# Later value loads, output ids behind the branch, a hint on the branch, and expert weights one load earlier

## The chip, the core and the metric

The kernel runs on one core of a Trainium2 chip. TensorE (PE), VectorE (DVE), ScalarE (ACT), GpSimd (POOL) and SyncE (SP) are its engines; each has its own instruction stream, and they wait for each other by semaphores. SP issues the loads of q, k and v, POOL issues the loads of expert weights and the gathers and scatters of token rows. The metric is the device time of one execution in microseconds, the median of the runs; lower is better.

## The reference

Two stages follow each other. The first is causal attention over 4 batches, 8 heads, 768 positions and 64 dimensions, in which a query sees the 96 latest positions and 8 global ones, with a linear bias in the distance. The second is a balanced mixture of 8 experts over the 3072 rows of 512 values that attention gives:

```python
logits = x @ w_gate
order = np.argsort(-logits.flatten())        # all (token, expert) pairs, best first
for idx in order:                            # greedy
    tok, e = int(idx) // E, int(idx) % E
    if assigned[tok] >= 0 or counts[e] >= cap:
        continue                             # cap = 3072 / 8 = 384
    assigned[tok] = e
    counts[e] += 1
for e in range(E):
    mask = assigned == e
    out[mask] = np.maximum(x[mask] @ w1[e], 0.0) @ w2[e]     # 512 -> 1024 -> 512
```

Each token goes to exactly one expert, and each expert has exactly 384 tokens.

## The kernel before

**Attention, 0 to about 125 us.** The work is cut into eight units (a batch and four heads) and sixteen half-units n (a pair of heads). The order of all its instructions is written out by hand in two lists, `PROLOGUE` and `ORDER` (L540 to L560), of steps such as `S1` (scores), `BI`, `EX` (bias, exponential), `AV0` and `AV1` (the two parts of P times V, L405) or `KT`, `QT` (transposes of raw k and q). Raw q and k of a unit land in one of five slots (`load`, L264); v of a half-unit, in one of four (`load_v`, L272: five DMAs, 420 KB). All go through SP's queue in the order in which the lists reach them. A v slot is free again when `AV1` of its half-unit is done, and the load of half-unit n + 4 is written right behind it (L619).

**Routing, about 125 to 159 us.** Four rounds assign most pairs; `dispatch` then turns each token's expert and rank into lists of ids by matmuls with one-hot matrices: `idi` (L916, L930), by which rows are gathered from the token rows in DRAM, and `ido` (L925, L933, L934), by which results are scattered. `fill` puts matmuls of no use between them. A flag `fm` (L937) says whether the rounds left something over, so that the general path is needed; it isn't for these inputs. All engines read it and branch over the general path (L1194, L1195). The gathers of expert 0 are issued ahead of the branch, those of expert 1 behind it.

**Experts, from about 159 us.** Per expert e there are three slabs of 128 tokens. A slab is gathered (`gather`, L1086, nine slots `xe`), transposed by PE (`pxe`, L1107) and copied to SBUF by DVE (`xT`, L1112). The hidden layer is 32 matmuls (`ph`, L1136; expert 0 by slabs, L1126), ACT's relu writes `hT` (L1139), the output layer is 8 matmuls for each slab (`po`, L1169), DVE copies it to one of four `ot` (L1173), and POOL scatters it to `out_dram` (L1174). Behind expert 0's and e's hidden layer the slabs of the next expert are transposed between the slabs of the output layer. The weights of experts 0 to 2 are loaded earlier; `late_weights` (L707) issues w1 and w2 of experts 3 to 7, 1 MB each, one at each expert, two at expert 0 (L1144, L1146), behind the gathers of expert e + 2. A scheduler sets the order between engines' independent instructions here, while `keep_in_program_order` pins what the code marks. In the tables below, s0, s1, ... are the scatters in order, three for an expert.

Of the kernel before, what the change touches and what calls it, by code (L numbers as in the profile page):

```python
# [9 lines left out]
FP32 = mybir.dt.float32  # L10
# [10 lines left out]
DM = H_ * D_  # L21
# [18 lines left out]
TOP = 64  # L40


@with_exitstack
def kernel(
# [173 lines left out]
    with ExitStack() as actx:  # L218
# [342 lines left out]
        VLOAD = {"S0:0": 1, "S1:0": 2, "S2:0": 3}  # L561
        pss = {}
# [14 lines left out]
        def step(op, u):  # L577
# [36 lines left out]
            elif k == "AV":  # L614
                if op[2] == "0":
                    attend(n, (0, 1, 2, 3), 0)
                else:
                    attend(n, (2, 3, 4, 5, 6), 1)
                    if n + NB < 2 * NU:  # L619
                        load_v(n + NB)  # L620
# [39 lines left out]
        with tc.manual_schedule():  # L660
# [4 lines left out]
            nc.sync.dma_start(wg_sb, moe_w_gate.rearrange("(kc p) e -> p kc e", p=128))  # L665
# [5 lines left out]
            load("q", 1)  # L671
            load_v(0)
# [44 lines left out]

    idi = consts.tile([128, NCHUNK], I32)
    ido = consts.tile([128, NCHUNK], I32)
    fm = consts.tile([1, 1], FP32)  # L720

    def routing(general):
      with ExitStack() as dctx:
        dap = dctx.enter_context(tc.tile_pool(name="dap", bufs=1))
        ohp = dctx.enter_context(tc.tile_pool(name="ohp", bufs=1))
# [142 lines left out]
        def dispatch(d0=()):  # L868
# [29 lines left out]
            OH = ditp.tile([128, NCHUNK, NCHUNK], FP16, tag="OH", name="OH")  # L898

# [7 lines left out]
            ohl_of = []  # L907
            for q_, m in enumerate((6, 6, 6, 4, 2)):
                ohl = ohp.tile([128, 128, m], FP16, tag=f"ohl{q_}", name=f"ohl{q_}")
                c0 = len(ohl_of)  # L910
                nc.vector.tensor_tensor(out=ohl, in0=iota_m[:, :, 0:m], in1=bc_m(lo[:, c0 : c0 + m], 128), op=ALU.is_equal)
                ohl_of += [ohl[:, :, i] for i in range(m)]
                if c0:
                    fill(1)
                for c in range(c0, c0 + m):
                    nc.tensor.matmul(pI, lhsT=ohl_of[c], rhs=OHr[:, :, c], start=(c == 0), stop=(c == NCHUNK - 1))  # L916
            assert not toks0 and (general or not toksA and not toksD), (toksA, toksD)
            if general:
                take(OH, ohl_of)
# [8 lines left out]
            for dst, src in ((idi, pI), (ido, pO)):  # L928
                if dst is idi:
                    nc.vector.tensor_scalar(out=idi, in0=src, scalar1=float(N_TOK // 2), scalar2=0.0, op0=ALU.add, op1=ALU.max)  # L930
                else:
# [302 lines left out]
```

## Time and profile before

| | |
|---|---|
| median of 3 runs | 265.55 us (265.2, 265.55, 265.85) |
| profiled execution | 265.26 us |
| its span, first to last instruction | 263.3 us |
| PE, DVE, ACT, POOL busy | 90%, 56%, 58%, 58% |
| mean granted clock of PE | 0.969 of full speed |
| POOL's DMA queue (software_dynamic) | 26.22 MB, 49.5% of 16 engines' span |
| SP's DMA queue (hardware_dynamic) | 22.50 MB, 31.6% |
| instruction DMAs (q8 and q14) | 39 packets, 0.50 MB |

The time is that of the whole execution; the profile's times count from its first instruction. Busy shares are means over three stages with different limits. A chain of waits goes back from the last instruction to what released each step; "issue" in it is time in which an engine waited for nothing that the profile shows. The granted clock is given as a share of 2.4 GHz, so 0.50 is 1.2 GHz. The kernel's inputs are the same in every run, so the branch goes the same way each time.

### The profile page before, as it was taken

What the parts mean: (1) busy time and instruction counts of PE and PEld (TensorE: products, weight loads), DVE (VectorE), ACT (ScalarE), POOL (GpSimd) and SP (SyncE); (2) the same over time, 40 slices, a digit from 0 to 9 for tenths busy, and PEclk for the clock granted to TensorE, in tenths of its full rate; (3) what the DMA queues carried; (4) which work ended last, traced back from release to release, by engine and by line L of the source; (5) the groups of instructions that cost most, each with busy time, mean ns of one, the idle gap of its engine ahead of it and who ended that gap; (6) DMA issues with size and microseconds to landing.
All of it is one profiled execution on the core that took longest, in us unless ns stands there. A gap on an engine that the chain in (4) does not pass through costs nothing. (4 is left out here: it accounts for less than half of the span.)

```text
span 263.3 us, 6939 instructions
## 1 busy us (share of the span) xinstructions
PE 236.5 (90%) x2746; PEld 166.5 (63%) x2757; DVE 147.7 (56%) x330; ACT 153.4 (58%) x301; POOL 153.6 (58%) x285
## 2 busy tenths in 40 slices
PE   8599899799998999999788895999999499999991
PEld 3477778587786888877677664755655245555550
DVE  3999989488898966564878851232121323141320
ACT  1858899399889898464889811532505023505230
POOL 6546948849939989978210027881677572222412
PEclk9889999799999999999999999999999689999998
DMA  6999999764573499999997524599999999417803
GB/s 244 332 415 262 217 250 303 180 175 89 176 128 82 76 179 202 205 181 190 210 213 191 184 77 112 106 200 227 259 234 181 266 257 177 174 40 150 191 21 119
DMA packets 49895, 49.22 MB, mean 187 GB/s; under 512 B 29377, under 2 KB 41409, under 8 KB 49857
## 3 DMA queue, kind: packets, MB, share of 16 engines
q0 software_dynamic: 15712, 26.22, 49.5%
q1 hardware_dynamic: 34144, 22.50, 31.6%
q8 instruction: 23, 0.38, 0.6%
q14 instruction: 16, 0.12, 0.1%
HBM read 56.05 MB, written 9.44 MB: 249 GB/s over the span
## 5 line engine op out<-in xcount | busy, mean ns | idle before, releaser
L1139 ACT ACTIVATE hT<-ph 128x384 bf16<-128x384 f32 x56 | 27.5, 491 | 56.7 <-PE ph L1136 56.2
L365 DVE SCALAR_TENSOR_TENSOR P<-Dm,ps 128x432 f32<-128x432 f32 x92 | 49.2, 598 | 10.1 <-PE ps L347 10.1
L372 ACT ACTIVATE P<-P 128x864 f32<-128x864 f32 x48 | 42.7, 923 | 8.2 <-DVE P L365 7.5
L1173 DVE COPY ot<-po 128x512 f32<-128x512 f32 (+1 forms) x24 | 16.1, 675 | 51.8 <-PE po L1169 27.5
L1086 POOL DMA_INDIRECT xe<-x_tok,idi x24 | 24.3, 1014 | 33.9 <-DVE fc L937 20.0
L1174 POOL DMA_INDIRECT out_dram<-ot,ido x24 | 23.8, 990 | 34.7 <-DVE ot L1173 28.8
L384 POOL TENSOR_TENSOR S<-P 128x576 f32<-128x576 f32 (+1 forms) x32 | 38.9, 1215 | 8.3 <-ACT P L372 7.1
L405 PE MATMUL po<-P,v 128*64 128x216 f32 (+6 forms) x576 | 43.3, 300 | 0.1
L405 PEld LDWEIGHTS po<-P,v 128*64 128x64 f32 x576 | 35.9, 141 | 9.9 <-issue 2.6
L287 DVE STREAM_TRANSPOSE arena<-w_early 128x768 f32<-128x768 f32 x32 | 30.0, 958 | 5.1 <-DMA w_early<-in_k_dram 3.5
L1169 PEld LDWEIGHTS <-hT 128*128 128x128 bf16 x200 | 19.4, 101 | 20.7 <-issue 3.3
L295 ACT COPY kA<-arena 128x720 f32<-128x720 f32 (+2 forms) x18 | 23.6, 1340 | 6.0 <-DVE arena L287 6.0
L347 PE MATMUL ps<-qT,kA 32*128 32x216 f32 (+2 forms) x448 | 23.7, 335 | 3.4 <-DVE P L365 1.9
L519 ACT ACTIVATE x<-pw,ri 128x64 bf16<-128x64 f32 x112 | 24.5, 341 | 3.5 <-PE pw L504 3.5
L347 PE MATMUL ps<-arena,kA 32*128 32x216 f32 (+2 forms) x416 | 21.5, 342 | 4.6 <-ACT arena L315 2.7
L347 PEld LDWEIGHTS ps<-qT,kA 32*128 32x128 f32 x448 | 19.7, 185 | 6.0 <-issue 4.8
L347 PEld LDWEIGHTS ps<-arena,kA 32*128 32x128 f32 x416 | 18.3, 190 | 6.9 <-issue 3.7
L1112 DVE COPY xT<-pxe 128x512 bf16<-128x512 bf16 x24 | 9.5, 418 | 23.3 <-PE pxe L1107 18.3
L412 ACT COPY oT<-po 128x384 f32<-128x384 f32 x32 | 14.7, 475 | 13.4 <-PE po L405 13.4
L1169 PE MATMUL po<-w_late,hT 128*128 128x512 bf16 x69 | 18.4, 423 | 0.2
L1136 PE MATMUL ph<-xT,w_late 128*128 128x384 bf16 x96 | 16.1, 326 | 0.0
L422 PE MATMUL t<-S,onesx 128*32 128x192 f32 x256 | 13.7, 332 | 0.0
(186 smaller groups left out, 353.0 us busy)
## 6 DMA issues: line engine op xcount, KB each, us to landing
w_early<-in_k_dram SPq DMA_DIRECT2D x8, 768.0 KB
w_early<-in_q_dram SPq DMA_DIRECT2D x8, 768.0 KB
w_late<-in_moe_w_dram POOLq DMA_DIRECT2D x6, 1024.0 KB, 11.6
v<-in_v_dram SPq DMA_DIRECT2D x32, 180.0 KB
w_early<-in_moe_w_dram POOLq DMA_DIRECT2D x8, 512.0 KB, 8.9
w_last<-in_moe_w_dram POOLq DMA_DIRECT2D x4, 1024.0 KB, 11.0
arena<-in_moe_w_dram POOLq DMA_DIRECT2D x2, 1024.0 KB, 8.7
x_tok<-x SPq DMA_DIRECT2D x2, 768.0 KB
```

The costliest lines, as they stand in the source:

```text
L287: nc.vector.transpose(out=t, in_=raws[kind, u][:, :, 32 * g : 32 * g + 32])
L295: nc.scalar.copy(out=kAs[u % 2][:, g, i0:i1, 8:128].rearrange("p i (c j) -> p i c j", j=NJ), in_=t[:, i0 * NC5 : i1 * NC5, :].rearrange("p ...
L347: nc.tensor.matmul(at(a)[:, o : o + w], lhsT=kA[r, gd, i, :], rhs=qTt[r, gd, KT * i : KT * i + w], start=(gd == 0), stop=(gd == 1), skip_g ...
L365: nc.vector.scalar_tensor_tensor(out=Ps[n][:, 2 * g : 2 * g + 2, t, :], in0=W, scalar=-8.0 * slopes[2 * (n % NPAIR) + t], in1=st[:, 0 : 2 ...
L372: nc.scalar.activation(P, P, AF.Exp, scale=0.125)
L384: nc.gpsimd.tensor_tensor(out=to[:, :, :, 0:OV], in0=P[:, i0 : i0 + m, :, 0:OV], in1=P[:, i0 - 1 : i0 + m - 1, :, KT:QW], op=ALU.add)
L405: nc.tensor.matmul(po[n, bank][64 * t : 64 * t + 64, a - QB * bank : z - QB * bank], lhsT=v7[:, t, i, :], rhs=Ps[n][:, min(i, 5), t, a - q ...
L519: nc.scalar.activation(x[:, 2 * hf + i, 128 * jj + 64 * t : 128 * jj + 64 * t + 64], ps[:, i, 64 * t : 64 * t + 64], AF.Identity, scale=ri ...
L1086: tc.keep_in_program_order(nc.gpsimd.indirect_dma_start(out=xes[s], out_offset=None, in_=x_tok[:, :], in_offset=bass.IndirectOffsetOnAxis( ...
L1139: nc.scalar.activation(hT[:, fc, :], ph, AF.Relu)
L1169: pin(e, nc.tensor.matmul(po[:, lo:hi], lhsT=hT[:, t, fc, :] if e == 0 else hT[:, fc, 128 * t : 128 * t + 128], rhs=w2_of(e)[:, fc, lo:hi] ...
L1174: s = nc.gpsimd.indirect_dma_start(out=out[:, :], out_offset=bass.IndirectOffsetOnAxis(ap=ido[:, TSLAB * e + t : TSLAB * e + t + 1], axis= ...
```

## The change

There are five parts.

1. Loads of v. A table `VNEXT` says behind which `AV1` a v load stands. v4 now follows `AV1` of half-unit 2, not 0; v5 that of 3, v6 that of 4, v7 and v8 that of 5, and so on, up to v15 behind 11, where it was. The load of the gate weights `wg_sb` moves behind q1.
2. Output ids. The 24 matmuls for `ido` and DVE's two instructions on them leave `dispatch` and stand behind the branch: 14 matmuls ahead of the first slab's transposes, 10 behind them. The fillers there and those between the matmuls are dropped.
3. The branch. The general path is the block that is preferred as fallthrough, and a hint for its branch, "LikelyTaken", is marked for PE, DVE, ACT and POOL in `dispatch`. In the built program the hint is the first instruction of these four engines' programs, more than 300 ahead of the branch, and the few instructions of the other side stand behind the general path instead of ahead of it.
4. The first slab's copy to `xT` is ACT's.
5. The first half of w1 of expert 4 is loaded ahead of expert 1's gathers, the second half and w2 of expert 4 behind them; the second `late_weights` at expert 0 goes. Each later load so stands one step earlier.

```diff
+        VNEXT = {2: (4,), 3: (5,), 4: (6,), 5: (7, 8), 6: (9,), 7: (10,), 8: (11,), 9: (12, 13), 10: (14,), 11: (15,)}
...
                     attend(n, (2, 3, 4, 5, 6), 1)
-                    if n + NB < 2 * NU:
-                        load_v(n + NB)
+                    for m in VNEXT.get(n, ()):
+                        load_v(m)
...
-            nc.sync.dma_start(wg_sb, moe_w_gate.rearrange("(kc p) e -> p kc e", p=128))
             load("k", 1)
...
             load("q", 1)
+            nc.sync.dma_start(wg_sb, moe_w_gate.rearrange("(kc p) e -> p kc e", p=128))
             load_v(0)
...
+    def late_half(hf):
+        m, e = lates[0]
+        assert m == 0
+        tc.keep_in_program_order(nc.gpsimd.dma_start(
+            w1_of(e)[:, 2 * hf : 2 * hf + 2, :],
+            moe_w1[e].rearrange("(kc p) f -> p kc f", p=128)[:, 2 * hf : 2 * hf + 2, :]))
+        if hf:
+            lates.pop(0)
...
+            if not general:
+                tc.mark_branch_hint_location("general", "LikelyTaken", engines=HINT)
...
-            pO = ps_d.tile([128, NCHUNK], FP32, tag="pr", name="pO")
-            for c in range(NCHUNK):
-                if c % 6 == 0:
-                    fill(2)
-                nc.tensor.matmul(pO, lhsT=ohl_of[c], rhs=OH[:, :, c],
-                                 start=(c == 0), stop=(c == NCHUNK - 1))
...
                     if e == 0 and t == 0:
-                        pw = ps_o.tile([128, DM], FP32, tag="po", name="pw")
-                        for i in range(2):
-                            pin(0, nc.tensor.matmul(pw, lhsT=ident_bf, rhs=w1_of(0)[:, 0, 0:DM], start=(i == 0), stop=(i == 1)))
-                    nc.vector.tensor_copy(out=xT_of[e][:, :, t, :], in_=pxe)
+                        out_ids(14, NCHUNK)
+                        pin(0, nc.scalar.copy(out=xT_of[e][:, :, t, :], in_=pxe))
+                    else:
+                        nc.vector.tensor_copy(out=xT_of[e][:, :, t, :], in_=pxe)
...
+            def out_ids(c0, c1):
+                for c in range(c0, c1):
+                    pin(0, nc.tensor.matmul(pO, lhsT=ohl_of[c], rhs=OH[:, :, c], start=(c == 0), stop=(c == NCHUNK - 1)))
+
+            def ido_out():
+                idf = fp.tile([128, NCHUNK], FP32, tag="idf", bufs=1, name="idf")
+                pin(0, nc.vector.tensor_scalar(out=idf, in0=pO, scalar1=float(N_TOK // 2), scalar2=0.0, op0=ALU.add, op1=ALU.max))
+                pin(0, nc.vector.tensor_scalar(out=ido, in0=idf, scalar1=float(N_TOK - 1), scalar2=None, op0=ALU.min))
...
                 late_weights()
-                if e == 0:
-                    late_weights()
-                if e == 0:
-                    pw = ps_h.tile([128, 512], FP32, tag="ph", name="pw")
-                    for i in range(3):
-                        pin(0, nc.tensor.matmul(pw, lhsT=ident_bf, rhs=w1_early[:, 0, 0, 0:512], start=(i == 0), stop=(i == 2)))
...
                 if e == 0:
+                    out_ids(0, 14)
                     load_x(0, (0,))
+                    ido_out()
...
-    with tc.If(flag > 0, preferred_fallthrough_block=False):
+    with tc.If(flag > 0, preferred_fallthrough_block=True, label="general"):
         routing(True)
+    late_half(0)
     gather(1)
+    late_half(1)
+    late_weights()
     experts()
```

POOL's program from the branch on, before: six gathers (three for expert 1, three for expert 2) stand ahead of the first two weight loads, which are w1 and w2 of expert 4.

```order
249 L1195 UNCONDITIONAL_BRANCH
250 L1086 DMA xe_3209<-x_tok,idi 128x512
251 L1086 DMA xe_3213<-x_tok,idi 128x512
252 L1086 DMA xe_3217<-x_tok,idi 128x512
253 L1086 DMA xe_3230<-x_tok,idi 128x512
254 L1086 DMA xe_3234<-x_tok,idi 128x512
255 L1086 DMA xe_3238<-x_tok,idi 128x512
256 L714 DMA w_late_1930<-in_moe_w_dram 128x4x1024
257 L714 DMA w_late_1931<-in_moe_w_dram 128x8x512
258 L1086 DMA xe_3446<-x_tok,idi 128x512
```

And after it; `128x2x1024` is half of w1 of expert 4.

```order
249 L1205 UNCONDITIONAL_BRANCH x2
250 L725 DMA w_late_1930<-in_moe_w_dram 128x2x1024
251 L1089 DMA xe_3123<-x_tok,idi 128x512
252 L1089 DMA xe_3127<-x_tok,idi 128x512
253 L1089 DMA xe_3131<-x_tok,idi 128x512
254 L725 DMA w_late_1930<-in_moe_w_dram 128x2x1024
255 L718 DMA w_late_1931<-in_moe_w_dram 128x8x512
256 L1089 DMA xe_3147<-x_tok,idi 128x512
257 L1089 DMA xe_3151<-x_tok,idi 128x512
258 L1089 DMA xe_3155<-x_tok,idi 128x512
259 L718 DMA w_late_1932<-in_moe_w_dram 128x4x1024
260 L1184 DMA out_dram<-ot,ido 3072x512
```

The first half has moved ahead of expert 1's gathers, the rest of expert 4's weights ahead of expert 2's, and w1 of expert 5 ahead of expert 3's gathers and of the first scatter.

SP's loads at the start of the second slots' use, before (`v7_0` and `v7_1` are the slots that take v4 and v5 here; the q and k are of later units).

```order
31 L268 DMA w_early_99<-in_q_dram 128x1536
32 L277 DMA v7_0_137<-in_v_dram 120x6x64
33 L279 DMA v7_0_137<-in_v_dram 8x7x64
34 L277 DMA v7_0_137<-in_v_dram 120x6x64
35 L279 DMA v7_0_137<-in_v_dram 8x7x64
36 L281 DMA v7_0_137<-in_v_dram 48x2x64
37 L268 DMA w_early_99<-in_k_dram 128x1536
38 L277 DMA v7_1_138<-in_v_dram 120x6x64
```

And after.

```order
31 L271 DMA w_early_99<-in_q_dram 128x1536
32 L271 DMA w_early_99<-in_k_dram 128x1536 x2
33 L271 DMA w_early_99<-in_q_dram 128x1536
34 L280 DMA v7_0_137<-in_v_dram 120x6x64
35 L282 DMA v7_0_137<-in_v_dram 8x7x64
36 L280 DMA v7_0_137<-in_v_dram 120x6x64
37 L282 DMA v7_0_137<-in_v_dram 8x7x64
38 L284 DMA v7_0_137<-in_v_dram 48x2x64
39 L280 DMA v7_1_138<-in_v_dram 120x6x64
```

Two loads of k and one of q now stand ahead of v4.

DVE at the branch, before: the two instructions that make `ido` stand between the flag and the branch.

```order
211 L930 TENSOR_SCALAR idi<-pI 128x24
212 L936 TENSOR_REDUCE fc_2517<-pf 1x8
213 L937 TENSOR_SCALAR fc_2517,fm<-fc_2517 1x8
214 L933 TENSOR_SCALAR idf<-pO 128x24
215 L934 TENSOR_SCALAR ido<-idf 128x24
216 L1194 TENSOR_LOAD fm
217 L1195 COMPARE_AND_BRANCH
```

And after, with the general path left out.

```order
212 L937 TENSOR_SCALAR idi<-pI 128x24
213 L939 TENSOR_REDUCE fc_2484<-pf 1x8
214 L940 TENSOR_SCALAR fc_2484,fm<-fc_2484 1x8
215 L1204 TENSOR_LOAD fm
216 L1205 COMPARE_AND_BRANCH
...
324 L1205 UNCONDITIONAL_BRANCH x2
325 L1129 TENSOR_SCALAR idf<-pO 128x24
326 L1130 TENSOR_SCALAR ido<-idf 128x24
327 L1115 COPY xT_3175<-pxe 128x4x128 x2
```

DVE reads the flag right behind its making; the two instructions stand behind the branch, ahead of two copies of slabs instead of three.

## Rows read from the trace of the kernel before

**Rows 1.** Busy time, share of the span and instructions of PE, from the page.
```profile
PE 236.5 (90%) x2746; PEld 166.5 (63%) x2757; DVE 147.7 (56%) x330; ACT 153.4 (58%) x301; POOL 153.6 (58%) x285
```

**Rows 2.** The chain that ended last: start us, us, what.
```profile
158.93 2.83 issue
...
162.40 1.05 PE ph L1126 x16
...
179.41 0.45 PE pxe L1107 x8
...
195.84 10.60 DMA out_dram<-ot,ido
...
208.22 5.95 PE po L1169 x16
...
214.16 5.20 PE ph L1136 x32
...
232.81 3.45 PE po L1169 x16
```

**Rows 3.** Timeline of PE at the stand: start us, busy us, instructions, idle before.
```profile
207.63 0.59 PE L1107 MATMUL pxe<-ident_bf,xe 128*128 128x128 bf16 x4 [3.94 <-DVE xT L1112]
```

**Rows 4.** Window behind it: length, busy of five engines, PEclk, DMA share, GB/s.
```profile
206.30:213.10 6.80, 5.47 (x16) 2.19 (x16) 2.98 (x6) 0.00 (x0) 5.07 (x5) 0.50 1.15 200
```

**Rows 5.** PE's timeline at 48 us; DMA queue from 45.4 to 45.5 us.
```profile
48.23 1.00 PE L347 MATMUL ps<-qT,kA 32*128 32x216 f32 x13 [1.34 <-issue]
...
q8 instruction: 1, 0.02, 83.8%
```

**Rows 6.** Windows in attention: all engines, then PE and PEld for L405 alone.
```profile
44.00:46.00 2.00, 2.00 (x43) 1.51 (x42) 2.00 (x4) 2.00 (x4) 2.00 (x7) 1.00 1.27 186
...
49.65:53.70 4.05, 3.96 (x36) 3.11 (x36) 0.62 0.45 174
...
65.70:68.30 2.60, 2.51 (x36) 2.12 (x36) 1.00 0.72 272
```

**Rows 7.** Timeline of POOL, which issues the expert stage's DMAs.
```profile
167.29 1.81 POOL L714 DMA_DIRECT2D w_late<-in_moe_w_dram  x2
...
191.05 1.00 POOL L1086 DMA_INDIRECT xe<-x_tok,idi  x1 [0.30 <-PE pxe L1107]
...
192.35 1.00 POOL L1086 DMA_INDIRECT xe<-x_tok,idi  x1 [0.30 <-issue]
...
193.66 1.04 POOL L1174 DMA_INDIRECT out_dram<-ot,ido  x1 [0.30 <-DVE ot L1173]
...
194.70 0.83 POOL L714 DMA_DIRECT2D w_last<-in_moe_w_dram  x1
...
203.77 0.96 POOL L714 DMA_DIRECT2D w_last<-in_moe_w_dram  x1
```

**Rows 8.** Landing times of DMAs issued at 158.48, 167.29/168.1, 191.05, 192.35, 193.66, 194.70, 203.77.
```profile
DMA to landing us min/median/max: 4.1/4.1/4.1
...
DMA to landing us min/median/max: 8.5/11.6/14.6
...
DMA to landing us min/median/max: 7.6/7.6/7.6
...
DMA to landing us min/median/max: 6.7/6.7/6.7
...
DMA to landing us min/median/max: 6.0/6.0/6.0
...
DMA to landing us min/median/max: 11.0/11.0/11.0
...
DMA to landing us min/median/max: 10.9/10.9/10.9
```

**Rows 9.** Timeline of PE ahead of the branch: six of the out ids' matmuls.
```profile
157.35 0.44 PE L925 MATMUL pO<-OH,ohl 128*128 128x24 f16 x6
```

**Rows 10.** Timeline of SP, which issues the loads of q, k and v.
```profile
48.03 0.35 SPq L268 DMA_DIRECT2D w_early<-in_q_dram  x1
```

More of the change, by code (lines that the diff above doesn't have):

```diff
@@ L40 @@
 TOP = 64
+HINT = (mybir.EngineType.PE, mybir.EngineType.DVE, mybir.EngineType.Activation, mybir.EngineType.Pool)
 @with_exitstack
@@ L720 @@
     fm = consts.tile([1, 1], FP32)
+    idp = ctx.enter_context(tc.tile_pool(name="idp", bufs=1))
+    OH = idp.tile([128, NCHUNK, NCHUNK], FP16, name="OH")
+    PIECES = (6, 6, 6, 4, 2)
+    ohls = [idp.tile([128, 128, m], FP16, name=f"ohl{i}") for i, m in enumerate(PIECES)]
+    ohl_of = [ohls[i][:, :, j] for i, m in enumerate(PIECES) for j in range(m)]
     def routing(general):
@@ L724, in routing @@
         dap = dctx.enter_context(tc.tile_pool(name="dap", bufs=1))
-        ohp = dctx.enter_context(tc.tile_pool(name="ohp", bufs=1))
         rpool = ditp = dctx.enter_context(tc.tile_pool(name="rpool", bufs=1))
@@ L897, in dispatch @@
             fill(5)
-            OH = ditp.tile([128, NCHUNK, NCHUNK], FP16, tag="OH", name="OH")
             def bc_m(t, m):
@@ L906, in dispatch @@
             pI = ps_d.tile([128, NCHUNK], FP32, tag="rk", name="pI")
[L907 to L910, printed above, removed]
+            if not general:
+                tc.mark_branch_hint_location("general", "LikelyTaken", engines=HINT)
+            c0 = 0
+            for ohl, m in zip(ohls, PIECES):
                 nc.vector.tensor_tensor(out=ohl, in0=iota_m[:, :, 0:m], in1=bc_m(lo[:, c0 : c0 + m], 128), op=ALU.is_equal)
-                ohl_of += [ohl[:, :, i] for i in range(m)]
                 if c0:
@@ L916, in dispatch, with take @@
                     nc.tensor.matmul(pI, lhsT=ohl_of[c], rhs=OHr[:, :, c], start=(c == 0), stop=(c == NCHUNK - 1))
+                c0 += m
             assert not toks0 and (general or not toksA and not toksD), (toksA, toksD)
             if general:
-                take(OH, ohl_of)
+                take()
             nc.vector.tensor_tensor(out=OH, in0=OH, in1=bc_m(idt, NCHUNK), op=ALU.mult)
-            pO = ps_d.tile([128, NCHUNK], FP32, tag="pr", name="pO")
-            for c in range(NCHUNK):
-                if c % 6 == 0:
-                    fill(2)
-                nc.tensor.matmul(pO, lhsT=ohl_of[c], rhs=OH[:, :, c],
-                                 start=(c == 0), stop=(c == NCHUNK - 1))
-            fc8 = dap.tile([1, N_EXP], FP32, name="g_fc" if general else "fc8")
[L928 to L931, printed above, removed]
-                    idf = ditp.tile([128, NCHUNK], FP32, tag="idf", name="idf")
-                    nc.vector.tensor_scalar(out=idf, in0=src, scalar1=float(N_TOK // 2), scalar2=0.0, op0=ALU.add, op1=ALU.max)
-                    nc.vector.tensor_scalar(out=dst, in0=idf, scalar1=float(N_TOK - 1), scalar2=None, op0=ALU.min)
-                if dst is idi and not general:
-                    nc.vector.tensor_reduce(out=fc8, in_=pf.rearrange("p (c e) -> p e c", e=N_EXP), axis=AX.X, op=ALU.add)
-                    nc.vector.tensor_scalar(out=fc8, in0=fc8, scalar1=float(CAP), scalar2=None, op0=ALU.is_gt,
-                                            op1=ALU.add, accum_out=fm)
-        def take(OH, ohl_of):
+            fc8 = dap.tile([1, N_EXP], FP32, name="g_fc" if general else "fc8")
+            nc.vector.tensor_scalar(out=idi, in0=pI, scalar1=float(N_TOK // 2), scalar2=0.0, op0=ALU.add, op1=ALU.max)
+            if not general:
+                nc.vector.tensor_reduce(out=fc8, in_=pf.rearrange("p (c e) -> p e c", e=N_EXP), axis=AX.X, op=ALU.add)
+                nc.vector.tensor_scalar(out=fc8, in0=fc8, scalar1=float(CAP), scalar2=None, op0=ALU.is_gt,
+                                        op1=ALU.add, accum_out=fm)
+        def take():
             for t in range(TSLAB):
@@ L1116, in pin @@
                     tc.keep_in_program_order(i_)
+            pO = ps_o.tile([128, NCHUNK], FP32, tag="po", name="pO")
+            def out_ids(c0, c1):
[5 more added lines that the diff above has]
+                pin(0, nc.vector.tensor_scalar(out=ido, in0=idf, scalar1=float(N_TOK - 1), scalar2=None, op0=ALU.min))
             def first_hidden(hT, t):
```

## The prediction

> **What bounds the kernel now.** I read the table of busy time first, then the chain of waits from its end backwards, then, at each gap in it, the timeline, the granted clock and the queue behind the gap. PE is busy 90% of the span [rows 1], so time can be won only where PE stands, where it works at the lower of its two clocks, or by work that leaves it. From 162.4 to the end the chain [rows 2] runs through PE, and the change touches two interruptions of it. The first is the branch: from 158.93 on, when DVE has compared, 2.83 us pass in which nothing that the profile shows is awaited; then the first slab is copied and PE begins expert 0. The second is a scatter, issued at 195.84 and landed 10.60 us later, at 206.4. DVE's next ot waits for it, the copy of a slab of expert 4 stands behind that ot on DVE, and PE stands for 3.94 us [rows 3]. Behind the stand the granted clock is 0.50, PE's lower level, for 6.8 us [rows 4]: sixteen po matmuls take 5.95 us, elsewhere 3.45 [rows 2]. So the place costs 3.9 + 2.5 and some 0.3 on the transposes: 6.7 us. A third place is in attention: at 46.9 PE stands 1.34 us for nothing visible [rows 5], and soon after it the same 36 matmuls take 3.96 us at clock 0.62 that take 2.51 at full clock [rows 6]: 1.34 + 1.45 = 2.8 us.
>
> **The weight queue, the largest term.** Weights, gathers and scatters of the expert stage go through POOL's DMA queue, and they land in the order in which they are issued. The gathers issued at 191.05 and 192.35 land 7.6 and 6.7 us later, at 198.65 and 199.05 (0.4 apart); the scatter of 193.66 at 199.7 (0.6 more); the 1 MB load of 194.70 at 205.7 (6.0 more); the scatter of 195.84 at 206.4 (0.7 more) [rows 2, 7, 8]. The next load, 203.77 + 10.9 = 214.7, lands 9.0 after the one before, with three gathers and three scatters between them: 9.0 − 1.2 − 1.95 = 5.85. Of the two loads issued in a row at 167.29 and 168.1, the first lands after 8.5, at 175.8, the second after 14.6, at 182.7: 6.9 apart. So a load costs 5.85, 6.0 or 6.9; I take 6.0, what it took right at the place in question, and keep 5.85 and 6.9 as bounds. A gather costs 0.4, a scatter 0.65.
>
> The change adds no bytes here. It moves every late load one step up: half a load goes ahead of expert 1's gathers, half behind them, and POOL issues the first when it leaves the branch, where before the first late load of this stage was issued at 167.29 [rows 7]. The last gather of expert 0 lands at 158.48 + 4.1 = 162.6 [rows 8], and from there the queue does not run dry. Up to and with scatter s5, the one that now stands where the scatter of 195.84 stood, there are six loads (36), fifteen gathers (6) and six scatters (3.9): s5 lands at about 162.6 + 45.9 = 208.5. From the landing to PE's next step it took 1.2 us before (206.43 to 207.63, an ot and a copy, [rows 2, 3]), so expert 4's hidden layer starts at 209.7, against 214.16 [rows 2]: −4.4. PE comes to that place at 203.7 (where it stood before) − 2.2 (head, below) + 1.5 (a wait for s4, which lands at 201.8 by the same sum) + 3.7 (the transposes and sixteen po at full clock) = 206.7, and stands 3.0 us there. One more wait, about 1.0, comes behind expert 4's po, since the next scatters now have loads in front of them too. Net −3.4, if the clock stays at its upper level.
>
> What is late next: expert 1's slabs land at 162.6 + 3 + 1.2 = 166.8, an estimated 1 us before they are wanted; expert 2's, behind one load more, at 166.8 + 9 + 1.2 = 177.0, wanted at 179.41 [rows 2] − 2.2 = 177.2. That cover is thin: if a load takes more than 6.0, PE waits there as well, though such a wait only uses up what it would stand later. Each 0.1 us on a load costs 0.6 at s5: at 5.85 the term is −4.3, at 6.55 it is gone, at 6.9 it is +2 before any clock.
>
> **The head.** The out ids' 24 matmuls (0.44 us per six, [rows 9]) and the eight fillers between them leave the stretch ahead of the branch, and DVE's two instructions behind them, so that DVE, the last at the branch, gets there about 2.3 us sooner. Behind it 14 of these matmuls (14 × 0.073 = 1.0) fit under the first gather's flight; ten more stand behind the first transposes, under ACT's copy. If the 2.83 us go on all engines, PE starts expert 0 at 160.2 instead of 162.4 [rows 2]; if they stay (the block jumped over now lies between the compare and what follows it, on the four engines too), they begin earlier and PE starts at 161.5. Neither counts: s4 and s5 land when the queue has worked through, and that begins with gathers issued ahead of the branch. A head later by up to 1.5 + 3.0 us only shortens the two stands. I enter 0; the bounds are −0.3 (a little of the last wait) and +1.0 (without fillers PE rests from 155 to 159, its clock falls, expert 0's matmuls take up to twice as long, and this eats the cover and a little more).
>
> The Trainium skill ("Runtime: NRT & Kernel Launch", section "Instruction fetch mechanics") says that prefetch is sequential only and that a taken branch out of the window waits for a fetch. The 2.83 us agree with such a fetch; by that rule a hint at the program's start would do nothing and the head would start at 161.5, with the same time at the end.
>
> **Attention.** In 44 to 46 the DMA engines are fully taken (share 1.27, [rows 6]) by SP's loads of v6 and v7. In a tenth of a microsecond at 45.4 one instruction packet holds 83.8% of 16 engines' time [rows 5], which is 0.838 × 16 × 0.1 = 1.34 us on its one engine, and PE's stand is 1.34. I read it as PE's next instructions held up among these loads. The change issues v4 and v5 where v6 and v7 were, and these two only behind q6 (48.03 before, [rows 10]). Two v loads are 0.84 MB, at 186 GB/s [rows 6] 4.5 us of queue that is not yet there at 45.4. v4 and v5 still are, and end about then; I take 0.3 of the stand as left: −1.0. Bounds: 0 (the packet meets v5 instead) and −2.8 (the stand and the slow clock behind it go). v4 lands at about 45, used at 49.7 [rows 6]; the later v loads keep their distance, as their slots bound them; the gate weights come one load later, where POOL isn't waited for: 0, at most +0.5.
>
> By the Trainium skill ("DMA: Bandwidth & Descriptors", section "Queues, rings and completion order") each DMA engine takes turns between its queues packet by packet, so that a fetch would not wait behind SP's backlog. By it this term is 0 and the sum 262.2; the row of 1.34 us speaks for contention, though not for which kind.
>
> **Sum.** −3.4 (queue) + 0 (head) − 1.0 (attention) = −4.4. The profiled execution took 265.26 us, a span of 263.3 and 1.96 around it, and is 0.29 under the median of 265.55. 265.26 − 4.4 = 260.86, and + 0.29 gives 261.2.
>
> **Rivals.**
> A2. The slow clock behind 49 us goes with the stand: another −1.45, 259.7. For it: the clock fell only after PE had stood. Against it: some stand may be left.
> B. The clock falls in the new stand of 3.0, as it did in that of 3.94. Sixteen matmuls' 2.5 us come back, of which the following wait of 1.0 takes a part: +1.8, 263.0. Against it: the new stand is shorter.
> C. Moving loads up only moves the waits: what s5 gains, later scatters and w2 loads lose, and attention's fetch meets v5. At 6.55 us a load this is what the sum gives: about 265.2. For it: the same bytes pass through one queue, which is the bound throughout.
> D. The slower end. Half a load and a whole one more stand ahead of expert 1's and 2's gathers, and a whole one ahead of s5. From 6.55 us a load on, PE stands at expert 1, 2 and 4, each time with the chance of the lower clock. At 7.0: 6 × 1.0 − 3.4 = +2.6, − 1.0 in attention, + 2 for one stretch of slow clock: +3.6, 269. For it: the 6.9 of the load at 168.1; against it: 5.85 and 6.0, nearer to the place.
> E. The hint doesn't do what it says: DVE's 2.83 us stay, PE starts at 161.5, and the time is still 261.2, since the head has slack. This is inside the first case.
>
> **How the numbers follow.** First case (with E) 0.40, its own range 260.2 to 262.4; A2 0.14; B 0.18; C 0.13; D 0.15. 0.3%, 0.8 us, is about what a measurement of this kernel can tell from no change, and C lies within it; the first case, A2 and B are faster: 0.72. The range goes from 257.8 (A2 with 5.85 a load, and the head's 0.3 or a shorter stand) to 265.2, which takes in B and half of C and leaves out D.
>
> **What would show it.** In the changed kernel's profile: a scatter that lands near 208.5, and expert 4's first matmul near 209.7; loads that land 6.0 apart on POOL's queue; expert 2's transposes without a wait; the granted clock behind PE's stand (the first case or B); PE's stand at 47 under 0.5 us; the idle time behind DVE's compare (E). I am wrong if loads take 6.5 and more, or if expert 4 starts less than 2 us earlier.

## The result, and the profile after

The changed kernel takes 258.52 us (median of 3 runs, 258.48 to 259.15) against 265.55: a ratio of 0.974, 95% interval 0.971 to 0.977, so −7.0 us. The forecast was 261.2, with a range of 257.8 to 265.2. The profiled execution has a span of 256.7 us against 263.3. First the page's row of busy time for it:

```profile
PE 231.6 (90%) x2735; PEld 165.4 (64%) x2744; DVE 146.9 (57%) x329; ACT 153.5 (60%) x302; POOL 154.7 (60%) x286
```

PE's busy time fell by 4.9 us [rows 1]. The 11 matmuls less are all fillers; at the 0.22 us of one matmul of 512 columns (sixteen po in 3.45) they are an estimated 2.4 us, and the other half is matmuls that take less time. PE's share of the span did not move, so the page says nothing of where the time came from. The same instruction in the two traces does. The token routing ends, with the last instruction that makes the overflow flag, at 152.18 instead of 155.43 (−3.25). Expert 1's hidden layer starts at 174.17; one row of the kernel before, from its chain of waits (start, us, what), gives the time to set beside it:

```profile
174.21 5.20 PE ph L1136 x32
```

So the 3.25 us are gone again by expert 1. Then the chain of the changed kernel (the same columns), from the branch on:

```profile
153.54 3.09 issue
156.63 0.81 PE pO L1125 x14
...
158.59 1.89 PE ph L1140 x16
...
174.17 5.20 PE ph L1150 x32
179.37 0.45 PE pxe L1110 x8
...
203.86 3.45 PE po L1179 x16
207.32 5.20 PE ph L1150 x32
...
249.26 0.70 DVE ot L1183
```

Expert 4's hidden layer starts at 207.32 instead of 214.16 [rows 2], −6.84, and that stays to the end (span −6.6). The row ahead of it answers to the one of 5.95 us: sixteen po matmuls in 3.45. The link of 10.60 us through a scatter has no successor in this chain. The gain thus has two halves: −3.25 ahead of the branch, and −3.6 in the expert stage, made of +3.2 from the branch to expert 1 (the head) and −6.8 from there to expert 4.

PE's timeline in attention (start, busy us, line, tile, count, idle before) shows the first half:

```profile
45.44 1.74 PE L350 MATMUL ps<-qT,kA 32*128 32x216 f32 x32
47.12 0.44 PE L507 MATMUL t<-ident,oT 128*128 128x128 f32 x2
47.48 2.51 PE L408 MATMUL po<-P,v 128*64 128x216 f32 x36
```

All 32 ps matmuls now stand in one row without idle time, and the 36 po matmuls behind them take 2.51 us: neither the 1.34 us stand [rows 5] nor the slow 3.96 [rows 6] is left. Windows of the changed kernel (length, busy us of PE, PEld, DVE, ACT, POOL with counts, granted clock, DMA share, GB/s) at four places:

```profile
46.00:48.00 2.00, 2.00 (x36) 1.49 (x30) 0.51 (x2) 1.96 (x3) 1.85 (x5) 1.00 0.54 136
155.20:161.90 6.70, 4.99 (x60) 4.88 (x61) 0.51 (x3) 1.25 (x3) 5.76 (x7) 0.50 0.79 166
203.60:207.40 3.80, 3.80 (x23) 1.85 (x21) 1.39 (x3) 0.00 (x0) 1.88 (x3) 1.00 1.07 254
170.00:245.00 75.00, 74.68 (x460) 41.80 (x464) 21.85 (x42) 26.35 (x54) 40.82 (x41) 1.00 0.84 194
```

In attention the DMA share behind 46 is 0.54. At expert 4 the clock is 1.00 where it was 0.50 [rows 4]. Over 75 us of experts PE is busy for 74.68. A price is in the second row: the granted clock is 0.50, the lower of its two levels (1.2 GHz), over expert 0's first matmuls. PE had rested ahead of them, as its timeline shows:

```profile
156.63 0.81 PE L1125 MATMUL pO<-OH,ohl 128*128 128x24 f16 x14 [5.05 <-issue]
```

What the engines did at the branch is in the list of its line's instructions (engine, operation, duration in ns min/median/max, start in us); the compare is the instruction that reads the flag and branches, and an engine's event is its first step behind it; PE's rows are those of PEldq:

```profile
L1205 ACTq COMPARE_BRANCH  x1: 68/68/68, 152.8 to 152.8; - x1
...
L1205 PEldq COMPARE_BRANCH  x1: 3429/3429/3429, 152.9 to 152.9; - x1
L1205 DVEq COMPARE_BRANCH  x1: 84/84/84, 152.9 to 152.9; - x1
L1205 ACTq EVENT_SEMAPHORE  x1: 17/17/17, 153.3 to 153.3; - x1
L1205 DVEq EVENT_SEMAPHORE  x1: 21/21/21, 153.5 to 153.5; - x1
L1205 POOLq COMPARE_BRANCH  x1: 70/70/70, 154.0 to 154.0; - x1
L1205 POOLq EVENT_SEMAPHORE  x1: 17/17/17, 154.5 to 154.5; - x1
L1205 PEldq EVENT_SEMAPHORE  x1: 51/51/51, 156.4 to 156.4; - x1
```

ACT, DVE and POOL are through in 0.5 to 0.6 us; PE, hinted as well, spends 3.43 us in its compare. DVE's 2.83 [rows 2] are gone, and PE's 3.43 have come.

Yet the head's 3.2 us do not arise there. Expert 0's first matmul starts at 158.59 instead of 162.40 [rows 2], 3.81 earlier, so 0.56 are won up to it beside attention's 3.25. Its hidden layer, from that matmul to the first po, then takes 9.56 us instead of 5.80 (162.40 to 168.20). PE's rows of its second half, and one of ACT's:

```profile
163.36 1.50 PE L1140 MATMUL ph<-xT,w_early 128*128 128x128 bf16 x24
165.47 0.61 PE L1140 MATMUL ph<-xT,w_early 128*128 128x128 bf16 x8 [0.60 <-ACT hT L1143]
...
167.71 0.61 PE L1140 MATMUL ph<-xT,w_early 128*128 128x128 bf16 x8 [0.87 <-ACT hT L1143]
168.15 1.89 PE L1179 MATMUL po<-w_early,hT 128*128 128x512 bf16 x7
```
```profile
165.03 0.38 ACT L1143 ACTIVATE hT<-ph 128x256 bf16<-128x256 f32 x1 [1.31 <-PE ph L1140]
```

From 158.59 to 161.9 the clock is at half, an estimated 1.65 of the 3.76 us. The other 2.1 or so come behind that, at the upper clock: PE waits for ACT's relu, and ACT gets PE's signal only at 165.03, for a row of matmuls that began at 163.36.

Last, DVE's timeline around expert 4, where ot waits for scatters, and the first late load on POOL's:

```profile
196.62 0.69 DVE L1183 COPY ot<-po 128x512 f32<-128x512 f32 x1 [2.97 <-DMA out_dram<-ot,ido]
...
205.35 0.69 DVE L1183 COPY ot<-po 128x512 f32<-128x512 f32 x1 [2.49 <-DMA out_dram<-ot,ido]
...
207.03 0.69 DVE L1183 COPY ot<-po 128x512 f32<-128x512 f32 x1 [0.66 <-DMA out_dram<-ot,ido]
```
```profile
156.21 0.80 POOL L725 DMA_DIRECT2D w_late<-in_moe_w_dram  x1
```

The load starts 11.1 us earlier than before [rows 7]. The place at expert 4 hung on the scatter of 195.84, which landed at 206.4; now it hangs on a later one, s5 (issued at 194.59), and the ot that waits for it goes at 205.35. DVE still waits for scatters, but PE comes to this place at 207.3 and no longer notices: the stand of 3.94 [rows 3] has no counterpart.

### The profile page after: what moved, and what is told of

It is laid out like the page before. It is cut to its first block, busy times and chain, and to the rows that moved or that the text cites. A ratio compares the mean times of both kernels' runs of the same rounds, so it can differ in the third digit from the quotient of the medians.

```text
span 256.7 us, 6918 instructions
## 1 busy us (share of the span) xinstructions
PE 231.6 (90%) x2735; PEld 165.4 (64%) x2744; DVE 146.9 (57%) x329; ACT 153.5 (60%) x302; POOL 154.7 (60%) x286
## 5 line engine op out<-in xcount | busy, mean ns | idle before, releaser
L375 ACT ACTIVATE P<-P 128x864 f32<-128x864 f32 x48 | 42.6, 922 | 8.2 <-DVE P L368 7.9
L408 PE MATMUL po<-P,v 128*64 128x216 f32 (+6 forms) x576 | 41.9, 294 | 0.0
L408 PEld LDWEIGHTS po<-P,v 128*64 128x64 f32 x576 | 34.9, 137 | 9.2 <-issue 2.7
L1179 PEld LDWEIGHTS <-hT 128*128 128x128 bf16 x200 | 18.7, 98 | 18.8
L1179 PE MATMUL po<-w_late,hT 128*128 128x512 bf16 x69 | 16.0, 379 | 0.2
```

Of the source, the lines that this page charges most:

```text
L375: nc.scalar.activation(P, P, AF.Exp, scale=0.125)
L408: nc.tensor.matmul(po[n, bank][64 * t : 64 * t + 64, a - QB * bank : z - QB * bank], lhsT=v7[:, t, i, :], rhs=Ps[n][:, min(i, 5), t, a - q ...
L1179: pin(e, nc.tensor.matmul(po[:, lo:hi], lhsT=hT[:, t, fc, :] if e == 0 else hT[:, fc, 128 * t : 128 * t + 128], rhs=w2_of(e)[:, fc, lo:hi] ...
```

## The experiments

Each group of four ran on one chip, together with the kernel before; the chips differ (the kernel before took 265.06, 260.88 and 264.06 us on them), so times are compared within a group only, and ratios are to the kernel before on the same chip. In the first group e2_hint3 stands for the changed kernel: its trace has the same times at the branch, within 0.1 us.

**First group.** e1_v_old: the changed kernel with the old order of the value loads.

```
-                    for m in VNEXT.get(n, ()):
-                        load_v(m)
+                    if n + NB < 2 * NU:
+                        load_v(n + NB)
```

> The changed kernel with v loaded again behind AV1 of half-unit n - 4; all else as changed (gate weights behind q1 too). Theory 1: the later v loads alone gave attention's 3.25 us, because they took two loads out of SP's queue ahead of one instruction packet. Then PE stands again for about 1.3 us near 47, the clock falls near 49, idi is made 3.2 us later, and as everything behind hangs on that, the time is 258.5 + 3.2 = 261.7. Rival: the stand depended on something else that the change moved (the gate weights' load); then no stand, clock 1.00 at 50 us and 258.5.

260.78 us, 0.984 (0.981 to 0.988), 2.4 above e2_hint3. PE's timeline has the stand again:

```profile
46.62 1.36 PE L350 MATMUL ps<-qT,kA 32*128 32x216 f32 x19
48.82 1.00 PE L350 MATMUL ps<-qT,kA 32*128 32x216 f32 x13 [0.84 <-issue]
```

It breaks at the same place, after 19 of the 32 matmuls. Here the clock behind it stayed at 1.00, as it did in e10 below, whose stand at this place was 2.15 us long: a stand here does not always bring the slow stretch. Of the 2.4 us this trace has 1.5 between 41 and 51 us; another 1.1 arise at 16 to 24 us, where the edit does nothing, from the place at which an early slow stretch fell in this execution. So the old order of the value loads brings the stand; their share is 1.5 to 2.4, without the slow stretch.

e2_hint3: the hint without PE.

```
-HINT = (mybir.EngineType.PE, mybir.EngineType.DVE, mybir.EngineType.Activation, mybir.EngineType.Pool)
+HINT = (mybir.EngineType.DVE, mybir.EngineType.Activation, mybir.EngineType.Pool)
```

> The changed kernel with the hint on DVE, ACT and POOL alone. In the changed kernel these three leave the compare within 0.6 us, PE, which has the hint too, after 3.43, SP, without one, after 3.1. Theory 2: the hint did PE harm: without it PE leaves within 1 us as before the change, PE's first matmul is near 153.9 instead of 156.63, the clock stays 1.00 at the head, expert 0 ends 3 to 5 us earlier, but the scatters then hold PE at expert 4 (s5 landed at 205.3, so expert 4 not before 206.5 instead of 207.3): 257.7 or, with a slow clock in the new stand, 259. Rival: PE's jump needs its fetch with or without a hint: 3.4 us again, 258.5.

258.41 us, 0.975 (0.972 to 0.979). PE's compare:

```profile
L1205 PEldq COMPARE_BRANCH  x1: 3382/3382/3382, 152.9 to 152.9; - x1
```

3.38 us against 3.43: the hint does nothing for PE here.

e3_no_hint: no engine is hinted; the order of the blocks stays.

```
-            if not general:
-                tc.mark_branch_hint_location("general", "LikelyTaken", engines=HINT)
```

> The changed kernel without any hint, the block order as changed. Theory 3: the hint is what lets DVE, ACT and POOL leave in 0.5: without it each takes about 3 us like SP; PE as in the run with three hints. POOL's first half load then comes about 1 us later, DVE's semaphore near 156: PE begins near 156.5 either way, the time is 258.5 to 259.2. Rival: a hint at the start of the program does nothing and the block order alone made the three leave early: they leave in 0.5 again.

258.76 us, 0.977 (0.973 to 0.981). From its list of the branch's line:

```profile
L1203 DVEq COMPARE_BRANCH  x1: 72/72/72, 153.0 to 153.0; - x1
L1203 ACTq EVENT_SEMAPHORE  x1: 17/17/17, 153.3 to 153.3; - x1
...
L1203 DVEq EVENT_SEMAPHORE  x1: 21/21/21, 156.8 to 156.8; - x1
```

DVE needs 3.8 us instead of 0.6; ACT leaves as fast without the hint as with it (and POOL too, 154.1 to 154.6). The hint works, for DVE alone. Without it the time is only 0.3 us longer than e2's, hardly more than the runs scatter; that DVE matters so little here because ACT copies the first slab, and PE is held by its own compare (3.75 us in this run), is argued and not tested.

e4_late_old: the changed kernel with the late loads in their old places.

```
-    late_half(0)
     gather(1)
-    late_half(1)
-    late_weights()
...
                 late_weights()
+                if e == 0:
+                    late_weights()
```

> The changed kernel with the late loads in the old order (w1 and w2 of expert 4 behind expert 2's gathers). Theory 4: the stand at expert 4 went mainly because the queue now starts 3.25 us earlier and PE's head takes 3.2 us longer; the order of the loads gave little. By the old landing, 206.43 - 3.25 = 203.2, and 1.2 for ot and copy, PE has the slab at 204.4, wanted at 203.6: a stand of 0.8, no slow clock, 259.3. Rival: the order is worth the forecast 3.4 or more: 262 or later, with a stand of 3 us and more and the lower clock behind it.

262.02 us, 0.991 (0.988 to 0.995), 3.6 above e2_hint3. The number fits an expert stage bound by the queue, but the trace does not: PE never stands at expert 4, and all of it is lost at the head. Rows of ACT and of PE:

```profile
161.07 0.58 ACT L1113 COPY xT<-pxe 128x512 bf16<-128x512 bf16 x1 [11.71 <-remote]
```
```profile
161.71 1.89 PE L1140 MATMUL ph<-xT,w_early 128*128 128x128 bf16 x16 [3.32 <-issue]
```

ACT copies at 161.07 (157.95 in the changed kernel) what PE transposed by 157.96. So this run doesn't measure the queue.

**Second group.** e5_v_only: the kernel before with the new order of the value loads alone (the edit of e1 the other way round).

> The kernel before with the later v loads alone. Theory 1: PE doesn't stand near 47 and the clock stays up near 50, so idi is made 1.5 to 3.3 us earlier (the run with the old v loads lost 1.5 there and 1.1 to a slow clock at 16). Gathers and the queue behind them move with PE, so the stand at expert 4 stays 3.9 with its slow clock: 265.5 - 1.5 to 3.3 = 262.2 to 264. Rival: the v loads only matter beside the other parts: 265.5.

259.59 us, 0.998 (0.994 to 1.002). The routing ends at 152.5, as in the changed kernel, and expert 1's hidden layer starts at 171.36, 2.8 us sooner than in the changed one. Then PE's timeline:

```profile
203.47 0.38 PE L1108 MATMUL pxe<-ident_bf,xe 128*128 128x128 bf16 x4 [2.63 <-DVE xT L1113]
```

The stand at expert 4 is there, 2.63 us: the old load order sets when this place can start. But the clock behind this stand stays at 1.00, and expert 4's hidden layer starts at 207.31, where it starts at 207.32 in the changed kernel, on another chip: in these two traces the value loads alone reach the same time by another way. The kernel before took 260.88 on this chip and has no trace there, so how much of its stand and slow clock it had is not known; what the value loads win alone stays open. The next three, near to the whole change, are 1.0 to 1.7 us below this run.

e6_old_layout: the changed kernel with the general block laid out ahead, as before; the hint stays.

```
-    with tc.If(flag > 0, preferred_fallthrough_block=True, label="general"):
+    with tc.If(flag > 0, preferred_fallthrough_block=False, label="general"):
```

> The changed kernel with the order of blocks of before (the few instructions of the other side right behind the compare, the general path behind them), the hints kept. Theory 5: it is the order of blocks that gives PE its 3.4 us at the compare, since before the change PE left in 0.5: PE's first matmul near 153.9, at clock 1.00, expert 0's first layer 3 us earlier; the far jump of DVE takes 0.5 if its hint still serves, 2.8 as before if not, which then holds the start of expert 0 to about 156. The scatters hold expert 4 at 206.5 instead of 207.3, so the time is 257.7, or 259 to 260 if the clock falls in the new stand. Rival: PE's jump needs its fetch either way: 258.5.

258.60 us, 0.991 (0.987 to 0.996). PE's compares:

```profile
L1205 PEldq COMPARE_BRANCH  x2: 104/1610/3116, 152.9 to 153.3; - x2
```

3.1 us in the old layout too: the order of the blocks is not what made PE's branch dear. At expert 4 PE comes earlier here than in the changed kernel and stands 0.66 us for an ot that goes at 205.47.

e7_fill12: twelve filler matmuls on PE ahead of the branch.

```
+            fill(12)
             if general:
                 take()
```

> The changed kernel with twelve filler matmuls on PE between the ids' matmuls and the branch (12 x 0.22 = 2.6 us). Theory 6: the slow clock at the head comes from PE's rest of 5 us; with the fillers PE works until 154.2, compares then, leaves at 157.6 (1.0 later), rests 3.4 instead of 5.0. If the clock holds, expert 0's 3.4 us at half speed come back as 3.4 - 1.0 = 2.4 at the head, of which 0.8 can be won before the scatters hold PE: 257.7. Rival: a rest of 3.4 is enough for the slow clock: the head is 1.0 later: 259.5.

258.08 us, 0.988 (0.980 to 0.997). The compare, and PE's next rows:

```profile
L1206 PEldq COMPARE_BRANCH  x1: 861/861/861, 152.9 to 152.9; - x1
```
```profile
154.62 0.81 PE L1126 MATMUL pO<-OH,ohl 128*128 128x24 f16 x14 [0.30 <-PEq L1206]
157.74 0.59 PE L1111 MATMUL pxe<-ident_bf,xe 128*128 128x128 bf16 x4 [2.31 <-issue]
```

PE leaves in 0.86 us. In this run a 16 KB instruction packet was fetched at 151.3, ahead of the branch, in the changed kernel only at 153.9, behind its compare at 152.9. In the kernel before it came at 154.5, ahead of PE's compare at 157.5; in e6 at 154.1, behind it. This fits the length of PE's program ahead of the branch as the cause: the change moved 24 matmuls behind it and dropped 8 fillers, each with its weight load. But PE then waits 2.31 us at the transposes, the clock falls all the same (0.51 from 157.4 to 164.3), and expert 0 starts no earlier (159.05 against 158.59). The edit also changed POOL's built order: s5 is issued at 192.07, ahead of the load of 194.43, so this run does not test the queue's sum.

e8_half_behind: both half loads behind expert 1's gathers.

```
-    late_half(0)
     gather(1)
+    late_half(0)
     late_half(1)
```

> The changed kernel with both halves of w1 of expert 4 behind expert 1's gathers (three gathers of 0.4 change place with half a load). With all late loads in the old order the head lost 3.5 us: ACT's copy of the first slab waited until 161.0 for a signal of PE, whose transposes the record has done at 158.0, and the stand at expert 4 was gone all the same. Theory 7: that loss goes with the gathers of expert 1 being issued first: then it is here too, 262. Rival: it goes with the six gathers in a row or with the later loads: 258.5 here.

257.87 us, 0.992 (0.988 to 0.995), with e6 and e7 within 0.8 us of each other. PE's compare (3.50 us) and the low clock (154.1 to 160.9) are much as in the changed kernel, and yet expert 0's hidden layer takes 6.83 us instead of 9.56. PE does not wait for ACT in it:

```profile
162.91 2.84 PE L1140 MATMUL ph<-xT,w_early 128*128 128x128 bf16 x48
165.59 1.89 PE L1179 MATMUL po<-w_early,hT 128*128 128x512 bf16 x7
```

The half load ahead of the gathers is not shown to be the cause of those waits: e6 and e7 have it there and no such waits either. Their 8.13 and 8.27 us are, within 0.15, the 5.80 of before and half the time that the clock was low in them (to 163.5 and 164.2). At expert 4 PE comes earlier, and stands; PE's row and DVE's:

```profile
206.24 5.36 PE L1150 MATMUL ph<-xT,w_late 128*128 128x384 bf16 x32 [1.48 <-DVE xT L1115]
```
```profile
205.16 0.69 DVE L1183 COPY ot<-po 128x512 f32<-128x512 f32 x1 [5.24 <-DMA out_dram<-ot,ido]
```

The scatter s5 sets it free at 205.16, against 205.35 in the changed kernel: the queue's bound is there, and shows when PE arrives at 204.8 instead of 207.3. The clock stays at 1.00 behind this stand.

**Third group.** e9_after: the changed kernel again.

> The changed kernel again, as reference for the other three of this chip. Chips differ: on the one of the first four runs the kernel before took 265.1, on the one of the next four 260.9. All theories: 6 to 7 us under the kernel before where that stands at expert 4 with a slow clock (265), 2 to 3 under it where it takes 261.

258.99 us, 0.983 (0.976 to 0.989): 5.1 less than the kernel before, where 6 to 7 was expected. The next three are read against this number.

e10_late_only: the kernel before with the new load order alone (the edit of e4 the other way round).

> The kernel before with the late loads one step earlier, nothing else. Theory 8, the price list of the prediction: from gathers at 155.8 on, s4 lands near 201.8 and s5 near 208.5; PE goes through expert 3 without the old stand of 3.9 and waits for expert 4 from 207.4 to 209.7 instead of starting it at 214.16: 4.4 us under the kernel before (261.1 against 265.5), or 2 to 2.5 under it if the clock falls in that wait. Rival: the earlier order gives nothing by itself, the gain came from attention and the queue's earlier start: 265.

264.06 us, 1.000 (0.997 to 1.004). PE runs through expert 4 without a stand, and yet nothing is won; it starts expert 4 at 212.94, so late that the missing stand says little of the queue. DVE's timeline at the branch, then two rows of the branch's line:

```profile
159.56 0.18 DVE L942 TENSOR_SCALAR idf<-pO 128x24 f32<-128x24 f32 x1 [4.58 <-remote]
...
165.87 0.42 DVE L1121 COPY xT<-pxe 128x512 bf16<-128x512 bf16 x1 [5.92 <-issue]
```
```profile
L1202 PEldq EVENT_SEMAPHORE  x1: 51/51/51, 159.6 to 159.6; - x1
L1202 DVEq EVENT_SEMAPHORE  x1: 21/21/21, 160.5 to 160.5; - x1
```

Two things happen at the head. PE begins its compare at 157.0 and is past the branch only at 159.6 (0.3 us after its compare in the kernel before), and DVE gets PE's signal of the out ids, whose last matmul ended at 157.3, at that same instant. And DVE's jump takes from 160.6 to 165.87, 5.2 us, of which 2.83 were known [rows 2]: its 8 KB instruction packet comes at 163.8, 3.1 us behind the compare, while POOL's queue, with the half load in it, holds 99.2% of the DMA time from 160.7 to 163.7. In the kernel before, that queue held 40.2% during DVE's jump, and the packet came 0.95 behind the compare.

e11_v_late_defer: both load orders on the kernel before, and the last three late loads issued behind the outputs of experts 3 to 5.

```
-                late_weights()
-                if e == 0:
+                if e < 3:
                     late_weights()
...
                     scatters.append(s)
+                if e >= 3:
+                    late_weights()
```

> The kernel before with the later v loads, the late loads one step earlier, and w2 of expert 6 and both of expert 7 then behind the scatters of experts 3, 4 and 5; the head of before (out ids and fillers ahead of the branch, DVE's copy, no hint). Theory 9: the changed kernel's head costs 3.2 us (PE rests 5 us at the branch and expert 0 runs at half clock), hidden by the scatter that expert 4 would have waited for anyway. With w2 of expert 6 out of the way s5 lands near 199 and nothing holds PE: hidden layer of expert 1 at 170.9, and from there without a wait to the end: 3.2 under the changed kernel, 255.3 where that takes 258.5. Rival: the queue stays the bound, or the loads put off come too late for expert 6 or 7 (needed near 232 to 243): as the changed kernel or slower.

262.34 us, 0.996 (0.992 to 1.000). PE stands nowhere for more than 0.4 us in the experts, and the loss at the head is the same: PE is at the branch from 154.8 to 157.4, DVE's jump lasts from 158.5 to 163.50.

e12_defer_hint: e11 with the hint, for DVE alone, and the new order of the blocks.

```
+            if not general:
+                tc.mark_branch_hint_location("general", "LikelyTaken", engines=(mybir.EngineType.DVE,))
...
+    with tc.If(flag > 0, preferred_fallthrough_block=True, label="general"):
```

> As the run before, with the hint on DVE alone and the order of blocks of the change. DVE took 2.83 us behind its compare before the change, 0.5 with the hint, 3.8 in the run without one. Theory 9: without the scatters in the way the head counts, so DVE's 2.3 us count: the first hidden layer 2 us earlier, 253.3. Rival: PE's own jump takes 3.4 us in this order of blocks, as in six runs: then PE begins where it did and the time is as in the run before, 255.3, or up to 1 us slower.

259.22 us, 0.983 (0.974 to 0.992): 3.1 less than e11, and level with the changed kernel's 258.99. DVE at the branch:

```profile
L1208 DVEq COMPARE_BRANCH  x1: 84/84/84, 156.4 to 156.4; - x1
L1208 DVEq EVENT_SEMAPHORE  x1: 21/21/21, 157.0 to 157.0; - x1
```

0.6 us instead of 5.0. With a load begun ahead of the gathers the hint and the order of the blocks, which this edit changes together, are worth about 3 us; PE too is past its branch earlier (155.5 against 157.4), so how much of that is the hint's is not shown. In e3, where ACT made the first copy, the hint was worth 0.3. On this chip no variant beats the changed kernel; on the second it was not run.

## Why the prediction came out as it did

**Attention: the mis-sized term.** It was entered at −1.0 (0.3 of the stand left, the slow clock kept), with −2.8 as the far bound; it brought −3.25. This is the rival A2: both the stand and the slow stretch went. That the value loads bring the stand was right: e1 shows it. The reading by which it was priced was not. The 1.34 us are how long that 16 KB packet took (others of its size in the same trace took 0.88 to 1.26), and it was in at 46.77, before PE's stand began at 46.89; that the two durations are equal is chance. In e1 the packet took 1.32 us and the stand 0.84, in e10 1.53 and 2.15. What agrees in the three is that PE goes on 1.43 to 1.48 us after the packet is in, and that the packet starts at 45.4, 46.1 and 45.9 with the old value loads, but at 42.6 in the changed kernel. So PE, as far as three stands can show it, waits for instructions that come some 3 us late beside the old loads; what holds them is not shown. The stand's whole cost is also more than its idle time: from the first of the 32 ps matmuls to the transposes behind them it took 3.63 us (45.53 to 49.16) and takes 1.68 (45.44 to 47.12), 1.95 apart, which is why the 3.25 exceed the far bound. The slow stretch's 1.45 need not come with the stand, since the clock stayed up behind it in e1 and e10; that this execution had it, and the gain with it, is luck.

The Trainium skill ("DMA: Bandwidth & Descriptors", "Queues, rings and completion order") says that a DMA engine takes turns between its queues, a whole packet of descriptors at a time. The inference that a fetch would then not wait beside SP's loads, by which this term would be 0, does not fit e1; the rule itself no run here tests.

**The queue: its price right.** s5 was to land at 208.5, in a queue that begins with the gathers behind the routing. Shifted by the 3.25 that attention gave, that is 205.25; the ot that waits for it goes at 205.35, and in e8 at 205.16. So the sum of 45.9 us for six loads, fifteen gathers and six scatters held, and rivals C and D, which needed 6.55 us a load and more, fell. The changed kernel's profile lists no landing times for these loads, so that each took 6.0 is not shown.

**The stands that did not come: a size right in part by luck.** Forecast were 1.5, 3.0 and 1.0 us of waiting for the queue. By the sum that freed PE at 208.5 + 1.2; shifted, 206.45. PE arrived at 207.3, 0.9 later, so the end was set by PE and not by the queue. The expert stage gave −3.6, and −3.4 was forecast, but the route differs: the term's size came from the queue, and what bound was PE, whose head was 3.2 us longer. The 0.9 that PE came late stand where 1.0 of a further wait was forecast; that the two sizes agree so well is luck. The sentence that a later head only shortens the stands is what happened, up to its limit. e8 is the same stage with an earlier PE, and it stands 1.48 us there. Rival B had no stand in which the clock could fall; it did not fall behind the 1.48 of e8 or the 2.63 of e5.

**The head: 0 by luck of that cover.** DVE's way to the branch became 2.55 us shorter (158.7 to 152.9, less 3.25), forecast 2.3. The hint freed DVE, so rival E (that it does nothing) is wrong for DVE and right for PE, ACT and POOL. But the head was worked out for DVE alone, and expert 0 was to start 2.2 us sooner; beside attention's share it started 0.56 sooner. PE's own compare, which grew from 0.3 us to 3.4, stands in that stretch, but e7, where it takes 0.86, starts expert 0 no earlier, so what held the start is not shown. The 3.2 us were lost behind it, in expert 0's hidden layer: some 1.65 to the lower clock, which stood in the text only as a bound of +1.0, and 2.1 to PE's waits for ACT, which stood nowhere.

The Trainium skill ("Runtime: NRT & Kernel Launch", "Instruction fetch mechanics") says that prefetch is sequential only and that a taken branch out of its window waits for a fetch. PE agrees (3.43 us, and 0.86 where the packet came ahead, e7); hinted DVE does not (0.6 against 3.8).

**The sum.** Had attention given −1.0, PE would have reached expert 4 2.25 later and the total would have been near −4.8, the forecast's −4.4 within a few tenths. So the miss of 2.7 us is attention's 2.25 and small remainders.

**Open.** What the order of the late loads wins by itself, since e4 and e10 both lose at the head; why ACT got PE's signals late in expert 0's hidden layer in the changed kernel and not in e6, e7 and e8; why PE needs 2.6 us for its branch in e10 and e11, without an instruction packet of PE in that time; why PE's signals came some 3 us late in e4 and PE stood 2.31 in e7; and what the value loads win on a chip whose kernel before is already at 260.88. In e10, e11 and e12 the signal arrives at the moment when PE passes its branch (159.6, 157.4, 155.5), which names the place and not the cause.

## What to carry to other kernels

Price a queue by what one load, one gather and one scatter add to landing times in the trace, and set its result against the arrival of the engine that waits: the end is the later of the two, so terms on both sides of it do not add (here load order alone 1.000 where the whole gave 0.983; value loads alone 0.998 on a chip where three kernels near to the whole gave 0.988 to 0.992). When instructions are moved across a branch, work out the branch anew for every engine, the ones that lost instructions ahead of it above all. Beside a load begun early DVE's jump took 5.2 us instead of 2.83 (e10), so judge a hint and an early load together. And an engine's instructions can come late in straight code too: set the end of the packet beside the end of the stand before pricing it by a duration that happens to match.

## What the runs showed of the hardware that was not expected

- The same branch's compare cost PE from 0.3 us (the kernel before) to 3.9 (e9); the 0.86 of e7 and the 3.43 differ by twelve matmuls ahead of it and by when a 16 KB packet started (151.3, 153.9).
- PE went on 1.43 to 1.48 us after a late packet of its instructions was in (attention, in the kernel before, e1 and e10).
- A hint whose own instruction runs in the first microsecond of the program saved DVE 3.2 us of its branch at 153, and ACT and POOL passed in about 0.5 with and without it.
- A jump of DVE took 2.83 us with gathers in POOL's queue (40.2% of the DMA time during it) and 5.2 with a half-megabyte load there (99.2% over most of it).
- A stand of PE of the same kind was followed by the lower clock in the kernel before (0.62 behind 1.34 us) and not in e1 and e10 (1.00 behind 0.84 and 2.15 us).
